# Feed-forward in 18 tiles of 256 tokens across batch borders, the first two interleaved, and one more head pair of batch 1 computed the early way

## The chip, the cores and the metric

The kernel runs on one NeuronCore of a Trainium2 chip. The core has five engines with queues of their own: TensorE (PE in the profile; its weight loads are shown apart as PEld), VectorE (DVE), ScalarE (ACT), GpSimd (POOL) and SyncE (SP), which here issues all DMA transfers. Each engine takes its instructions in the order in which they were put into its queue and waits for semaphores of the others. The metric is the device time of one execution in microseconds.

## The reference

There are three stages: attention of two kinds that are added, a low-rank mix along the sequence, and a feed-forward network. B = 8 batches, H = 8 heads, S = 576 positions, D = 64, so 512 channels.

```python
q_d, k_d, v_d = (t.reshape(B, H, S // 4, 4, D).mean(axis=3) for t in (q, k, v))
out_d = softmax(q_d @ k_d.T / sqrt(D)) @ v_d            # pooled by four
out_up = np.repeat(out_d, 4, axis=2)
out_local = softmax(where(|i - j| < 4, q @ k.T / sqrt(D), -1e9)) @ v   # window of 7
x = (out_up + out_local).transpose(0, 2, 1, 3).reshape(B, S, 512)
xt = x.transpose(0, 2, 1)
u = x + (xt @ U @ V).transpose(0, 2, 1)                 # U: 576x32, V: 32x576
out = u + relu(u @ w_ch1) @ w_ch2                       # 512 -> 2048 -> 512
```

(Shortened; the maximum is subtracted ahead of each exponential, and 1e-9 is added to each sum.) U, V and the two weight matrices come in as float64, which the kernel converts itself.

## The kernel before

**The plan.** The kernel doesn't issue instructions as it goes. It makes a list of operations (`op`, with an engine, an assumed duration, what is read and written, and a priority), and `Plan.run` plays the list through a small model of the engines, which then fixes the order in each queue. Lower priorities go first when an engine has a choice. A pair of heads `hp` of batch `b` has priority 10 (4b + hp) and up; feed-forward matmuls have FILL + step (1000 and up), so they fill TensorE where attention has nothing ready. PH and PF are the assumed durations of a feed-forward group of twelve and of three matmuls.

**Feed-forward.** Every number of the products is split in a high and a low part of type fp32r (uH, uL, hH, hL, W1H, W1L, W2H, W2L), and a product is three matmuls: high by high, low by high and high by low. The tokens of a batch are cut in two tiles of TN = 288. A *step* is one tile with one of the NFC = 16 chunks of 128 hidden channels. `ffn1` (L888) does 4 x 3 matmuls into `ps_h`; ScalarE makes hH = relu (L895), VectorE hL (L896). `ffn2` (L911), LAG = 3 steps later, does four groups of three matmuls into four accumulators, one PSUM bank for each quarter e of the 512 output channels. After the last chunk of a tile, POOL adds uH and uL (L921), VectorE adds the accumulator (L924), and four stores go out (L927). The steps run batch by batch, tile by tile, chunk by chunk.

**Weights.** `load_w1` and `load_w2` bring 16 raw chunks each; `convert` (L341 to L354) turns float64 bits to high and low float32 parts: two copies on ScalarE, four operations on VectorE (L342, L344, L347, L349), one on POOL. The raw chunks use the three buffers "Pt", which the late attention's products Pt (L799) use as well. W2 lives where the early attention had its buffers: the operation "late" releases them when all early operations are done, and the steps from the fourth on wait for it.

**Attention, two ways.** Pairs with b * HP + hp < NE = 5 (all four of batch 0, the first of batch 1) go *early*: scores, transposes and products with v all on TensorE (`early_global`, `local_blocks`), before W2 is there. Batch 0 then goes through `early_mix`; the pair of batch 1 stores its x to DRAM (x_s) and is mixed later. All other pairs go *late* (`late_global`, `local_attn`): the scores on TensorE are passed through DRAM to another layout, the product with v runs as POOL multiplications (L799) and VectorE sums (L804), and the result is stored as x_s (L806). `mix_part` reads x_s back twice (xL, Y), multiplies by U on TensorE (L848), then by V (L863, one matmul for each tile of tokens), adds x (L866) and writes uH (L869) and uL (L871) of that pair's 128 channels. A tile can start when all four pairs of its batch are mixed; uH and uL have two buffers each.

**Loops.** Early attention of batch 0 and the first pair of batch 1, then the weights, U, the mix of the held early pair, the rest of batch 1, then the steps. The attention of batch b + 1 is put into the list ahead of the first step of batch b; the order in the queues comes from the plan.

Of the kernel before, what the change touches and what calls it, by code (L numbers as in the profile page):

```python
# [201 lines left out]
def attn_mix_ffn_kernel(ctx: ExitStack, tc, q, kp, vp, qT, kT, v, U, Ub, V, w1, w2, mask, band, eye, pat, pool, vw, vn, ident, outT):  # L202
    nc = tc.nc
# [10 lines left out]
    TN = 288  # L214
    NT = S // TN
    R = V.shape[0] // 4
    MP, MJ = U.shape[0], U.shape[1] // R
    LAG = 3
# [3 lines left out]
    PH, PF = 1.587, 0.398  # L222
# [3 lines left out]
    NE = 5  # L226
# [48 lines left out]
    ident_sb = const.tile([128, 128], F32, name="ident_sb")  # L275
# [15 lines left out]

    band_sb = early_pool.tile([128, NS * KL], BF16, name="band_sb")
# [40 lines left out]
    dma(lambda: nc.sync.dma_start(out=mask_sb, in_=mask), [], ["mask"], 35, 32)  # L333

# [72 lines left out]

    heads = [slice(hh * D, (hh + 1) * D) for hh in range(2)]
# [86 lines left out]
    def late_global(b, hp, up_s, prio):  # L495
# [39 lines left out]
        def t_mm():  # L535
            for hh in range(2):
                for c in range(2):
                    for a in range(2):
                        nc.tensor.transpose(view(pt[hh])[:, c, a * QH:(a + 1) * QH],  # L539
                                            Es[hh]()[:, a, c * QH:(c + 1) * QH], ident_sb[:QH, :QH])  # L540
        op(PE, 0.52, t_mm, ek + ["ident"], pt, prio)
# [13 lines left out]
        od = g([QH, 4, D], "od")  # L555
# [114 lines left out]
    def early_mix(b, hp, x, prio):  # L670
# [14 lines left out]
        for t in range(NT):  # L685
            pu = psum(ps_m, "ps_u", "m:x", 2)
            cuts = [(r, max(t * TN, 128 * r), min((t + 1) * TN, 128 * (r + 1))) for r in range(NS)]
            cuts = [x for x in cuts if x[1] < x[2]]

            def um(t=t, pu=pu, cuts=cuts):  # L690
                tsl = slice(t * TN, (t + 1) * TN)
                nc.tensor.matmul(pu()[:, :TN], stk(), Vst[:, tsl], start=True, stop=False)
                for r, c0, c1 in cuts:
                    nc.tensor.matmul(pu()[:, c0 - t * TN:c1 - t * TN], flat(r), ident_sb[:, c0 - 128 * r:c1 - 128 * r],
                                     start=False, stop=(r == cuts[-1][0]))
            op(PE, pw(prio) * 1.05, um, rd + [(stk, 0), (stk, 1), (stk, 2), "ident", "V0H", "V1H", "V0L", "V1L"], [pu], prio)
            uH, uL = u_of(b, t)
            act(TN, lambda uH=uH, pu=pu: nc.scalar.activation(uH()[:, hp, :], pu()[:, :TN], AF.Copy),
                [pu], [(uH, hp)], prio, 0.05)
            dve(TN, lambda uH=uH, uL=uL, pu=pu: nc.vector.tensor_tensor(  # L700
                out=uL()[:, hp, :], in0=pu()[:, :TN], in1=uH()[:, hp, :].bitcast(F32), op=ALU.subtract),
                [pu, (uH, hp)], [(uL, hp)], prio)
# [106 lines left out]
    u_bufs = {}  # L809

    def u_of(b, t):
        if (b, t) not in u_bufs:
# [238 lines left out]
```

## Time and profile before

| | us |
|---|---|
| three runs, median (lowest to highest) | 1037.83 (1037.47 to 1038.42) |
| the profiled execution: span from first to last instruction | 1036.6 |
| TensorE busy | 996.9 |
| POOL busy | 557.2 |
| VectorE busy | 529.8 |
| ScalarE busy | 388.0 |

The profile is of one execution, with the span as its own time; the medians of the runs are a little above it. In the tables of groups, a row gives source line, engine, operation, the tile written and those read, the shapes, the count, the busy time in us and the mean of one in ns, and then the time for which the engine sat idle just before these instructions, with what ended it. In a timeline a row is start, duration (us), engine, line, operation, tiles, shapes, count. A row of a window gives from:to, length, then busy time and count of PE, PEld, DVE, ACT and POOL, then the granted TensorE clock (1.00 is full), the share of the DMA engines in use, and GB/s. The page's digits are tenths of 40 equal slices of the span. Matmuls are pipelined, so the duration of one is a latency: the distance from start to start tells what each costs.

### The profile page before, as it was taken

The numbers are of one execution on the slowest core, as the hardware profiler recorded it, in microseconds if no ns is written. First come the engines' busy times: TensorE is split into PE (matmuls) and PEld (weight loads), VectorE is DVE, ScalarE is ACT, GpSimd is POOL, SyncE is SP. The second block draws the span as 40 slices with busy tenths as digits, with TensorE's granted clock in tenths as the row PEclk, the third lists the DMA queues.
The fourth block names the chain that finished last, engine by engine and source line by source line (L and its number), as shares of the span: only waits on it lengthen the run. The fifth ranks groups of instructions, "written<-read, shape, count | busy, mean of one in ns | idle before, by whom it ended". The sixth has DMA issues, their size and how long they took to land.

```text
span 1036.6 us, 26946 instructions
## 1 busy us (share of the span) xinstructions
PE 996.9 (96%) x10831; PEld 975.3 (94%) x10831; DVE 529.8 (51%) x1054; ACT 388.0 (37%) x1234; POOL 557.2 (54%) x567
## 2 busy tenths in 40 slices
PE   6778898999999999999999999999999999999998
PEld 5667888999999999999999999999999999999998
DVE  5997898655554545444475344534652544211111
ACT  3676554442443434443344244423443232111110
POOL 4854568788575656565585638762765625211010
PEclk9896999999999999999999999999999999999999
DMA  8866764753555545545555355624644242000000
GB/s 279 226 172 179 199 186 116 149 138 104 135 137 115 141 113 132 128 86 146 120 137 125 87 132 133 143 75 101 151 116 117 64 113 50 24 1 24 1 24 23
DMA packets 222612, 120.30 MB, mean 116 GB/s; under 512 B 175492, under 2 KB 198456, under 8 KB 222488
## 3 DMA queue, kind: packets, MB, share of 16 engines
q1 hardware_dynamic: 222488, 118.58, 45.5%
q8 instruction: 85, 1.39, 0.6%
q14 instruction: 39, 0.32, 0.1%
HBM read 87.78 MB, written 30.75 MB: 114 GB/s over the span
## 4 chain that ended last, share of the span: by engine, by line
PE 84%; DVE 7%; POOL 3%; issue 2%; DMA 2%; ACT 2%; SPq 0%; DVEq 0%; POOLq 0%; ACTq 0%
PE acc L911 36%; PE ps_h L888 35%; PE ps_a L552 2%; PE ps_b L719 2%; DVE c L347 2%; PE ps_hu L848 1%; DVE c L349 1%; PE ps_t L539 1%; DMA w2r<-in_W 1%; PE ps_b L726 1%; POOL Pt L799 1%; DVE c L342 1%; DVE c L344 1%; PE ps_a L484 1%; PE ps_v L431 1%
## 5 line engine op out<-in xcount | busy, mean ns | idle before, releaser
L911 PE MATMUL acc<-hH,W2H 128*128 128x288 f32 x1024 | 310.5, 303 | 0.0
L896 DVE SCALAR_TENSOR_TENSOR hL<-ps_h,hH 128x288 fp32r<-128x288 f32 x256 | 116.6, 455 | 378.6 <-ACT hH L895 378.0
L888 PE MATMUL ps_h<-uH,W1H 128*128 128x288 f32 x1024 | 304.3, 297 | 4.1 <-DVE hL L896 3.1
L911 PE MATMUL acc<-hH,W2L 128*128 128x288 f32 x1024 | 303.1, 296 | 2.6 <-POOL W2L L354 2.6
L888 PE MATMUL ps_h<-uL,W1H 128*128 128x288 f32 x1024 | 303.4, 296 | 1.2 <-POOL uL L871 1.2
L911 PE MATMUL acc<-hL,W2H 128*128 128x288 f32 x1024 | 302.6, 296 | 0.0
L888 PE MATMUL ps_h<-uH,W1L 128*128 128x288 f32 x1024 | 302.0, 295 | 0.0
L799 POOL TENSOR_TENSOR Pt<-vl,at 128x896 f32<-128x896 f32 (+1 forms) x135 | 233.4, 1809 | 115.1 <-DVE acc L804 61.1
L895 ACT ACTIVATE hH<-ps_h 128x288 fp32r<-128x288 f32 x256 | 105.1, 410 | 433.6 <-PE ps_h L888 433.5
L888 PEld LDWEIGHTS ps_h<-uH,W1H 128*128 128x128 f32 x1024 | 193.5, 189 | 5.4 <-DVE hL L896 3.8
L911 PEld LDWEIGHTS acc<-hH,W2L 128*128 128x128 f32 x1024 | 193.2, 189 | 3.5 <-POOL W2L L354 3.5
L888 PEld LDWEIGHTS ps_h<-uL,W1H 128*128 128x128 f32 x1024 | 193.4, 189 | 1.5 <-POOL uL L871 1.5
L911 PEld LDWEIGHTS acc<-hH,W2H 128*128 128x128 f32 x1024 | 193.3, 189 | 1.1
L888 PEld LDWEIGHTS ps_h<-uH,W1L 128*128 128x128 f32 x1024 | 193.7, 189 | 0.0
L911 PEld LDWEIGHTS acc<-hL,W2H 128*128 128x128 f32 x1024 | 193.7, 189 | 0.0
L804 DVE TENSOR_REDUCE acc<-Pt 128x128 f32<-128x1024 f32 (+1 forms) x135 | 144.7, 1103 | 4.7 <-POOL Pt L799 2.3
L871 POOL TENSOR_TENSOR uL<-xT,uH 128x288 fp32r<-128x288 f32 x56 | 44.1, 811 | 71.3 <-ACT uH L869 71.2
L921 POOL TENSOR_TENSOR o<-uH,uL 128x288 f32<-128x288 f32 x64 | 49.8, 816 | 54.2 <-DMA out_t<-o 54.2
L840 POOL TENSOR_TENSOR xL<-xL,xH 116x640 fp32r<-116x640 f32 x28 | 44.0, 1572 | 64.2 <-ACT xH L839 49.3
L510 POOL TENSOR_TENSOR vr<-vr 72x256 f32<-72x256 f32 x54 | 42.4, 785 | 46.9 <-DMA vr<-in_v 46.8
L793 ACT ACTIVATE Pt<-ul 128x128 f32<-128x128 f32 (+1 forms) x135 | 48.4, 441 | 21.3 <-DVE acc L804 20.0
L744 ACT ACTIVATE se<-ps_b 96x114 f32<-96x114 f32 x108 | 38.5, 357 | 47.1 <-PE ps_b L719 34.1
(129 smaller groups left out, 1106.9 us busy)
## 6 DMA issues: line engine op xcount, KB each, us to landing
vl<-in_vp SPq DMA_DIRECT2D x54, 240.0 KB
out_t<-o SPq DMA_DIRECT2D x64, 144.0 KB
w1r<-in_W SPq DMA_DIRECT2D x16, 512.0 KB
w2r<-in_W SPq DMA_DIRECT2D x16, 512.0 KB
Y<-x_s SPq DMA_DIRECT2D x112, 72.0 KB
gT<-in_kT SPq DMA_DIRECT2D x27, 291.0 KB
xL<-x_s SPq DMA_DIRECT2D x28, 280.0 KB
gq<-in_qT SPq DMA_DIRECT2D x27, 288.0 KB
```

Of the source, the lines that this page charges most:

```text
L510: pool_tt(256, lambda x=x: nc.gpsimd.tensor_tensor(out=x()[:, :, 0:2, :], in0=x()[:, :, 0:2, :], in1=x()[:, :, 2:4, :], op=ALU.add), [x], ...
L744: act(n * KL, lambda p=ps[hh], se=se, n=n, rows=rows: nc.scalar.activation(se()[rows, 0:n].rearrange("p r k -> p (r k)"), p()[rows, 0:n * ...
L793: act(n * D, lambda n=n, ps=ps, Pt=Pt: nc.scalar.activation(Pt()[:, :n, :, 7], ul()[:, ps, :], AF.Copy), [ul], [(Pt, 1)], prio, 0.16)
L799: nc.gpsimd.tensor_tensor(out=Pt()[:, :n, :, 0:7].rearrange("p s d o -> p o s d"), in0=win, in1=at()[:, ps, :].rearrange("p s o -> p o s") ...
L804: dve(8.5 * n * D, lambda n=n, ps=ps, Pt=Pt: nc.vector.tensor_reduce(out=acc()[:, ps, :], in_=Pt()[:, :n], axis=AX.X, op=ALU.add), [(Pt, 0 ...
L840: pool_tt(640, lambda: nc.gpsimd.tensor_tensor(out=xL(), in0=xL().bitcast(F32), in1=xH().bitcast(F32), op=ALU.subtract), [xL, xH], [xL], prio)
L871: pool_tt(TN, lambda uH=uH, uL=uL, uf=uf: nc.gpsimd.tensor_tensor(out=uL()[:, hp, :], in0=uf(), in1=uH()[:, hp, :].bitcast(F32), op=ALU.su ...
L888: nc.tensor.matmul(ps()[:, :TN], w[:, dc, fs], u()[:, dc, :], start=(n == 0), stop=(n == 3 * NDC - 1))
L895: last_h[i] = act(TN, lambda: nc.scalar.activation(hH(), ps()[:, :TN], AF.Relu), [ps], [hH], FIRST, 0.05)
L896: dve(TN, lambda: nc.vector.scalar_tensor_tensor(hL(), ps()[:, :TN], 0.0, hH().bitcast(F32), op0=ALU.max, op1=ALU.subtract), [ps, hH], [hL ...
L911: nc.tensor.matmul(ac[e]()[:, :TN], W2[w][:, fc, es], hx(), start=(fc == 0 and n == 0), stop=(fc == NFC - 1 and n == 2))
L921: pool_tt(TN, lambda e=e, o1=o1: nc.gpsimd.tensor_tensor(out=o1()[:, :TN], in0=uH()[:, e, :].bitcast(F32), in1=uL()[:, e, :].bitcast(F32), ...
```

## The change

TN becomes 256 and tiles are numbered through all 8 x 576 tokens, so there are NG = 18 tiles of 256 and a tile may hold tokens of two batches. A batch's mix therefore writes its u in three pieces (`pieces`), and a tile waits for every pair of each batch that it touches (`parts`). Two quarters of an output tile share one PSUM bank; tiles take turns between two pairs of banks. The steps of the first two tiles alternate chunk by chunk. NE becomes 6, so the second pair of batch 1 goes the early way. uH and uL get three buffers. The final adds work on two quarters at once, with half as many stores (the last tile still by quarters). The identity used by the late transposes is a small tile of its own (`id_late`), the full one moves into the early memory. The assumed durations are set anew.

```diff
-    TN = 288
-    NT = S // TN
+    TN = 256
+    NG = B * S // TN
+    FIRST_TILES = 2
-    LAG = 3
+    LAG, HLB = 3, 3
-    PH, PF = 1.587, 0.398
+    PH, PF = 1.36, 0.34
-    NE = 5
+    NE = 6
-    ident_sb = const.tile([128, 128], F32, name="ident_sb")
+    id_late = const.tile([QH, QH], F32, name="id_late")
+    ident_sb = early_pool.tile([128, 128], F32, name="ident_sb")
+    dma(lambda: nc.sync.dma_start(out=id_late, in_=ident[0:QH, 0:QH]), [], ["id_late"], 35, 21)
+    def u_of(g):
+        if g not in u_bufs:
+            u_bufs[g] = (buf(ffn, [128, NDC, TN], F32R, "uH", bufs=3), buf(ffn, [128, NDC, TN], F32R, "uL", bufs=3))
+        return u_bufs[g]
+    def pieces(b):
+        cuts = [b * S] + [x for x in range(0, B * S, TN) if b * S < x < (b + 1) * S] + [(b + 1) * S]
+        return [(x // TN, x - b * S, y - x, x % TN) for x, y in zip(cuts, cuts[1:])]
+    parts = {}
+    for b in range(B):
+        for g, _, _, _ in pieces(b):
+            parts.setdefault(g, []).append(b)
...
-        for t in range(NT):
-            tsl = slice(t * TN, (t + 1) * TN)
+        for g, c, n, off in pieces(b):
             pu = psum(ps_m, "ps_u", "m:x", 2)
...
-            op(PE, 0.14, um, [(stk, 0), (stk, 1), (stk, 2), "V0H", "V1H", "V0L", "V1L"], [pu], prio)
+            op(PE, 0.13, um, [(stk, 0), (stk, 1), (stk, 2), "V0H", "V1H", "V0L", "V1L"], [pu], prio)
...
     def ffn1(s, i):
-        b, t, fc = s
-        uH, uL = u_of(b, t)
+        g, fc = s
+        uH, uL = u_of(g)
...
+        ur = [(u, c, b) for u in (uH, uL) for c in range(NDC) for b in parts[g]]
+        op(PE, PH, mm, ur + [f"W1_{fc}H", f"W1_{fc}L"] + ["late"] * (i >= HLB), [ps], FILL + i)
...
     def ffn2(s, i):
...
-            accs[(b, t)] = [psum(ps_acc, f"acc{e}", f"acc{e}", 1) for e in range(NDC)]
-        ac = accs[(b, t)]
+            accs[g] = [psum(ps_acc, f"acc{e}", f"acc{2 * (g % 2) + e}", 1) for e in range(NDC // 2)]
+        ac = accs[g]
+        half = lambda e: ac[e // 2]()[:, (e % 2) * TN:(e % 2 + 1) * TN]
...
-                    nc.tensor.matmul(ac[e]()[:, :TN], W2[w][:, fc, es], hx(),
-                                     start=(fc == 0 and n == 0), stop=(fc == NFC - 1 and n == 2))
+                    nc.tensor.matmul(half(e), W2[w][:, fc, es], hx(), start=(fc == 0 and n == 0 and e % 2 == 0),
+                                     stop=(fc == NFC - 1 and n == 2 and e % 2 == 1))
...
-    steps = [(b, t, fc) for b in range(B) for t in range(NT) for fc in range(NFC)]
+    first = [(g, fc) for fc in range(NFC) for g in range(FIRST_TILES)]
+    steps = first + [(g, fc) for g in range(FIRST_TILES, NG) for fc in range(NFC)]
...
+    for b in range(2, B):
+        attention(b)
     for i in range(len(steps) + LAG):
         if i < len(steps):
-            b, t, fc = steps[i]
-            if t == 0 and fc == 0 and b > 0 and b + 1 < B:
-                attention(b + 1)
             ffn1(steps[i], i)
```

105 lines of the change are left out of this document (51 added, 54 removed).

## The prediction

> **What bounds the kernel now.** I read the page first, for the engine that is busy and for the slices in which it isn't.
>
> ```profile
> PE 996.9 (96%) x10831; PEld 975.3 (94%) x10831; DVE 529.8 (51%) x1054; ACT 388.0 (37%) x1234; POOL 557.2 (54%) x567
> PE   6778898999999999999999999999999999999998
> DVE  5997898655554545444475344534652544211111
> PE acc L911 36%; PE ps_h L888 35%; PE ps_a L552 2%; PE ps_b L719 2%; DVE c L347 2%; PE ps_hu L848 1%; DVE c L349 1%; PE ps_t L539 1%; DMA w2r<-in_W 1%; PE ps_b L726 1%; POOL Pt L799 1%; DVE c L342 1%; DVE c L344 1%; PE ps_a L484 1%; PE ps_v L431 1%
> L911 PE MATMUL acc<-hH,W2H 128*128 128x288 f32 x1024 | 310.5, 303 | 0.0
> L888 PE MATMUL ps_h<-uH,W1H 128*128 128x288 f32 x1024 | 304.3, 297 | 4.1 <-DVE hL L896 3.1
> ```
>
> The chain that ended last is TensorE, 71% of it in the two feed-forward lines. Each line has three such groups of 1024, so the feed-forward is 6144 matmuls. The 303 and 297 ns are latencies of overlapped matmuls; what one costs is the distance between starts. For that I took the timeline in a stretch without attention, and a window that shows its clock:
>
> ```profile
> 959.81 0.29 PE L888 MATMUL ps_h<-uH,W1H 128*128 128x288 f32 x1
> ...
> 961.40 0.29 PE L911 MATMUL acc<-hH,W2H 128*128 128x288 f32 x1
> 950.00:1000.00 50.00, 50.00 (x380) 50.00 (x379) 8.32 (x19) 6.46 (x16) 3.14 (x4) 1.00 0.04 13
> ```
>
> Twelve matmuls lie between these starts: 1.59 us / 12 = 132.4 ns each, at a granted clock of 1.00 (in a window's row the third number from the right), while the other engines are nearly idle. So 6144 x 0.1324 = 813.5 us of the span of 1036.6 are feed-forward. The rest is the beginning and the attention's own matmuls.
>
> The second view is that beginning. Steps (a tile with one of the 16 weight chunks) 0 to 31 are the two tiles of batch 0; step 32 is the first that needs batch 1.
>
> ```profile
> L895 ACT ACTIVATE hH<-ps_h x32: 387/408/441, 85.0 to 223.7; 128x288 fp32r<-128x288 f32 x32
> L659 ACT ACTIVATE ob<-ps_ba x10: 418/431/438, 43.4 to 91.6; 128x320 f32<-128x320 f32 x10
> L351 ACTq EVENT_SEMAPHORE  x3: 17/38/38, 99.1 to 99.4; - x3
> L354 POOL TENSOR_TENSOR W2L<-c,W2H x16: 1263/1312/3420, 100.7 to 165.1; 128x512 fp32r<-128x512 f32 x16
> 105.00:165.00 60.00, 54.06 (x577) 51.43 (x576) 54.62 (x91) 31.55 (x87) 37.42 (x32) 0.97 0.65 182
> 195.06 0.52 SPq L806 DMA_DIRECT2D x_s<-acc  x1
> 209.72 0.34 SPq L806 DMA_DIRECT2D x_s<-acc  x1
> 229.35 0.29 PE L888 MATMUL ps_h<-uH,W1H 128*128 128x288 f32 x1
> 232.06 0.40 PE L888 MATMUL ps_h<-uL,W1H 128*128 128x288 f32 x1 [1.23 <-POOL uL L871]
> ```
>
> The early attention ends at 91.6; its memory is free for W2 at about 99. W2 is converted until 165.1, with VectorE busy 54.62 of 60 us. The raw weights and the attention's products Pt share three buffers, so the late pairs of batch 1 come through behind the weights: the second stores its x_s at 195.06, the third and last at 209.72. Step 32 starts at 229.35 (the 33rd hH follows the 32 above) and waits 1.23 us inside for uL. Up to here 32 steps of L888 and, with the lag of three, 29 of L911 are issued: 61 x 12 = 732 matmuls. The other 5412 x 0.1324 = 716.5 us; 1036.6 - 229.35 - 716.5 = 90.7 us are the late pairs from then on, their switches, and the end.
>
> So the sum for the new kernel has three terms: the start of step 32, the matmuls left (18 x 384 = 6912, less 732 = 6180) by their cadence, and some 91 us of others.
>
> **Term 1, the cadence at 256 columns.** The trace has no matmul of this shape. What stands near it:
>
> ```profile
> 92.43 0.44 PE L888 MATMUL ps_h<-uH,W1L 128*128 128x288 f32 x1
> 92.67 0.44 PE L888 MATMUL ps_h<-uH,W1H 128*128 128x288 f32 x1
> 92.19:94.59 2.40, 2.40 (x11) 2.40 (x11) 1.88 (x3) 0.98 (x4) 2.24 (x4) 0.50 0.55 149
> 891.76 0.46 PE L848 MATMUL ps_hu<-xH,Ust 116*64 116x128 f32 x5
> 892.06 0.46 PE L848 MATMUL ps_hu<-xL,Ust 116*64 116x128 f32 x5
> L888 PEld LDWEIGHTS ps_h<-uH,W1H 128*128 128x128 f32 x1024 | 193.5, 189 | 5.4 <-DVE hL L896 3.8 <-ACT ob L659 1.3
> L848 PEld LDWEIGHTS ps_hu<-xH,Ust 116*64 116x64 f32 x140 | 12.5, 135 | 2.7 <-POOL Ust L354 2.7
> ```
>
> At half the clock a matmul of 288 columns takes exactly 0.24 us, so 288 columns at full clock are 120 ns and 256 are 106.7; the measured 132.4 has a surplus of 12.4. A weight load of 128 columns takes 189 ns, of 64 columns 135: 54 ns per 64 columns, 108 per 128. L848 has 64 columns of weights and 128 of data and takes 0.30 us / 5 = 60 ns, 6 over its load of 54 and 7 over its columns (53.3). The new shape is L848 with both streams doubled: load 108, columns 106.7. From below 108 ns (a load per matmul), from above 106.7 + 12.4 = 119.1 (the surplus of 288 stays). Between them lies the line through 60 ns at 128 and 132.4 at 288: 0.4525 ns per column, 117.9 at 256. I take **114**: 108 + 6, as L848, the one row in which load and columns stand in the same proportion as in the new shape. 6180 x 0.114 = **704.5 us**.
>
> **Term 2, the start of step 32.** Three edits act here. *Two tiles together* gives TensorE two steps for every W2 chunk. *The second pair of batch 1 goes early*: one late pair less behind the weights. *Smaller tiles* shorten its 732 matmuls by 732 x 18 ns = 13 us.
>
> The extra early pair delays the release. Ten ob in five pairs from 43.4 to 91.6 is 12 us a pair at most (weight conversions ran between); I take 10, so W2 may be written from 109. Its VectorE work, from the groups of the first 210 us:
>
> ```profile
> L804 DVE TENSOR_REDUCE acc<-Pt 128x128 f32<-128x1024 f32 (+1 forms) x15 | 16.3, 1100 | 1.3 <-POOL Pt L799 1.1
> L451 DVE TENSOR_REDUCE mx<-ps_s 72x2 f32<-72x288 f32 x10 | 4.1, 446 | 2.3 <-PE ps_s L444 2.3
> L620 DVE TENSOR_REDUCE nm<-ps_b 128x5 f32<-128x190 f32 x10 | 3.2, 343 | 3.1 <-PE ps_b L600 3.1
> L622 DVE TENSOR_TENSOR ms_b<-ps_b,nm 128x190 f32<-128x190 f32 x10 | 3.2, 342 | 0.0
> L628 DVE TENSOR_REDUCE rs_b<-ms_b 128x10 f32<-128x380 f32 x5 | 2.7, 538 | 0.6 <-ACT ms_b L627 0.6
> L487 DVE TENSOR_TENSOR od<-ps_a,ri 72x128 f32<-72x128 f32 x10 | 2.8, 276 | 3.7 <-PE ps_a L484 3.6
> ```
>
> Two each of L451, L620, L622, L487 and one L628: 3.4 us, against 5 x 1.1 = 5.5 us of L804 alone for the late pair that goes. VectorE, the engine that limits the conversions, thus has no more to do; three chunks can be converted before the release, and only a little of the 10 us reaches the end of W2. Its loads and stores replace those of the late pair; the DMA engines' share was 0.65 in 105 to 165 (second number from the right in that window's row): hidden, and with that cover gone a few us of the same delay.
>
> Now batch 1's last pair is the second behind the weights: 195.06 + 1 for the later W2 + 21 from store to use (209.72 to 229.35, and the 1.23 waited) = **217**. TensorE alone would be there sooner: 109 + (732 - 36) x 0.114 = 188, plus three or four late pairs by the 90.7 us / 24 pairs = 3.8 us each, some 203. So what is late next is the attention, and TensorE waits up to 14 us, part of which other pairs' matmuls fill. Ends: 205 and 229 (nothing gained).
>
> **Term 3, the others.** 90.7 without the wait of 1.2; each of some 24 pairs gets three pieces of u instead of two (64, 128 and 192 columns among them): one more matmul, 108 to 132 ns by the rows above, 24 x 0.11 = 2.6: **92.1 us**. The third add, copy and subtract of each pair fall on engines at 51, 37 and 54%; the feed-forward covers them, and without that cover each pair would be under 2 us later. The accumulators of two tiles in turn remove a wait at the tile's border that the page shows as 0.0: nothing. The outputs (38 stores for 64, one wide add for two) and the smaller identity: nothing, TensorE goes on beside them. The last tile still stores by quarters: nothing.
>
> Two later places are tight. A tile then lasts 384 x 0.114 + 92.1 / 16 = 49.5 us. Tile 4 needs batch 2 at 217 + 99 = 316, tile 6 batch 3 at 415.
>
> ```profile
> L806 SPq DMA_DIRECT2D x_s<-acc x7: 337/344/530, 177.7 to 303.6; - x7
> L806 SPq DMA_DIRECT2D x_s<-acc x11: 332/344/530, 177.7 to 410.9; - x11
> ```
>
> Four pairs took 209.7 to 303.6, the next four to 410.9. From 196 on: batch 2 by 290 + 21 = 311, batch 3 by 397 + 21 = 418. That is cover of 5 us and a want of 3; a feed-forward step that waits there stands ahead of the attention's matmuls in TensorE's queue. From tile 9 on (564 against some 525) there is cover. I leave it at nothing and put it into the range.
>
> **Sum.** 217 + 704.5 + 92.1 = 1013.6 us of span. The median of the runs, 1037.83, is 1.2 over the profiled span: **1015 us**.
>
> **The rivals.**
>
> *A, the surplus stays (slower).* If the 12.4 ns belong to the matmul and not to its columns, 768 more matmuls pay them too: cadence 119.1, 6180 x 0.1191 = 736.0, span 1045.1, time **1046**. The place is every feed-forward matmul, and it decides from (1036.6 - 217 - 92.1) / 6180 = 117.7 ns on. For it: the cold row shows that columns alone cost 120. Against it: L848 has a surplus of 7. The Trainium skill, "TensorE: Matmul & The Clock Gate", section "Back-to-back issue gap", has this form, columns by the clock plus a constant 2.5 ns; the trace agrees with the columns at half clock and not with the constant (12.4), so its form speaks against the change and its size isn't this kernel's.
>
> *B, the line through the two rows.* 117.9 x 6180 = 728.6, span 1037.7, time **1039**. For it: two rows and no further assumption; against it: L848 may be paced by its load. This is the rival that I hold strongest, and it lies on the border of no change.
>
> *C, step 32 isn't earlier.* If the release and the weights slip as much as the pair saves, it stays at 229: 229 + 704.5 + 92.1, time **1027**. It is also what comes out when two tiles together do not fill TensorE. For it: VectorE has little room in 105 to 165.
>
> **Chances.** Forecast 0.56 (its own range 1002 to 1024, from step 32 at 205 to 225 and 112 to 115 ns), C 0.12, B 0.2, A 0.1, others 0.02. A measurement of this kernel can tell about 0.2%, 2 us, from none. Forecast and C are faster; B falls a quarter below 1035.8, a third within, the rest above; A is slower. Faster 0.74, same 0.07, slower 0.19. The range reaches from the forecast's lower end with a little more for the cadence's floor to B with some delay: 998 to 1043.
>
> **What would show it.** The distance of starts in L888 and L911 after attention has ended: 114 holds the forecast, 118 or more turns it. The first hH of tile 2 at about 217, with a wait on uL or uH before it and W2's last conversion at 165 to 170. Between 110 and 200 the steps of two tiles alternate and TensorE shows few gaps. Waits of L888 on the mix near 316 and 415, if the attention lags. I am wrong in size if the cadence is off by 1 ns (6.2 us), and in sign if it exceeds 117.7.

## The result and the profile after

The changed kernel takes **1066.23 us** in the median of four runs (1064.91 to 1070.98), the kernel before 1037.65 beside it: a ratio of **1.0277**, 95% interval 1.0247 to 1.0307. It is slower, and 51 us over the forecast. The profiled execution after has a span of 1062.7 us, so its median lies 3.5 us above it (1.2 before). One run of `plan_real_durations` (3340.61 us, its others 1069 to 1074) and one of the kernel before beside it (1899.37) stand far apart from the rest and are left out below.

The page of the kernel after: busy time, two rows of slices, and one group of each feed-forward line. ffn1 is now L899, ffn2 L923, hH L906, hL L907, ob L677.

```profile
PE 1004.9 (95%) x11706; PEld 984.8 (93%) x11706; DVE 532.2 (50%) x1088; ACT 398.5 (38%) x1294; POOL 539.8 (51%) x559
PE   5777498999999999999999999999999999999998
DVE  6887299665555544444445454645454443211111
L923 PE MATMUL acc<-hH,W2H 128*128 128x256 f32 x1152 | 332.9, 289 | 0.0
L899 PE MATMUL ps_h<-uH,W1H 128*128 128x256 f32 x1152 | 326.3, 283 | 2.2 <-DVE hL L907 2.2
```

TensorE is as full as before from the sixth slice on, and the feed-forward waits 2.2 us in all. The fifth slice shows a hole, a 4, with VectorE at 2. Both losses can be read from two further views. First the cadence, in the timeline of after where attention has ended:

```profile
954.35 0.28 PE L923 MATMUL acc<-hH,W2H 128*128 128x256 f32 x1
...
955.79 0.28 PE L899 MATMUL ps_h<-uH,W1H 128*128 128x256 f32 x1
...
957.20 0.28 PE L923 MATMUL acc<-hH,W2H 128*128 128x256 f32 x1
```

Twelve matmuls of L923 take 1.44 us, 120.0 ns each; twelve of L899 take 1.41, 117.5. Over all distances under 130 ns from step 32 on the means are 119.7 and 117.4, together 118.54, against 114 in the sum.

Second the beginning, by tiles of after (the third row answers for the first 245 us), with the start of step 32 from the timeline:

```profile
L677 ACT ACTIVATE ob<-ps_ba x12: 421/432/437, 41.4 to 117.7; 128x320 f32<-128x320 f32 x12
L354 ACT ACTIVATE W2H<-c x16: 612/632/637, 126.6 to 181.7; 128x512 fp32r<-128x512 f32 x16
L906 ACT ACTIVATE hH<-ps_h x35: 357/383/442, 86.6 to 241.3; 128x256 fp32r<-128x256 f32 x35
235.39 0.28 PE L899 MATMUL ps_h<-uH,W1H 128*128 128x256 f32 x1
```

The last early pair ends at 117.7 instead of 91.6, W2's first chunk is written at 126.6 instead of 100.0, and step 32 starts at 235.39, 6 us later than before and 18 later than forecast. The hole is the stretch from 105 to 128, in the windows of before and then of after:

```profile
105.00:128.00 23.00, 19.96 (x156) 19.11 (x155) 18.63 (x32) 11.79 (x33) 12.33 (x12) 0.99 0.76 213
```

```profile
105.00:128.00 23.00, 7.97 (x204) 6.84 (x205) 6.38 (x16) 7.45 (x25) 5.86 (x9) 0.50 0.68 166
127.00:235.00 108.00, 102.51 (x1154) 100.69 (x1147) 85.37 (x153) 57.00 (x171) 76.63 (x70) 0.99 0.59 149
```

TensorE and VectorE, at 20 and 18.6 us of these 23 before, now come to 8 and 6.4, and the granted clock stands at 0.50 (0.99 before). From 127 to 235 TensorE is nearly full again (102.5 of 108 us), so the delay stays. What the sixth pair waits for is in SyncE's part of the timeline of after, where a row's count is DMAs in a row and its length the time to issue them:

```profile
101.93 1.11 SPq L509 DMA_DIRECT2D up_e<-od  x2
...
106.06 3.22 SPq L845 DMA_DIRECT2D Y<-x_s  x4
109.40 2.23 SPq L400 DMA_DIRECT2D w2r<-in_W  x1
111.67 0.70 SPq L604 DMA_DIRECT2D vw<-up_e  x2
112.48 3.98 SPq L770 DMA_DIRECT2D s_s<-se  x8
...
121.75 1.36 SPq L683 DMA_DIRECT2D x_s<-ob  x1
```

and in TensorE's and ScalarE's (idle time before an instruction in brackets):

```profile
115.62 1.78 PE L673 MATMUL ps_ba<-vw,et 46*32 46x64 f32 x80 [4.31 <-DMA vw<-up_e]
125.69 0.26 ACT L794 ACTIVATE ms<-ms 128x63 f32<-128x63 f32 x1 [7.51 <-DVE ms L791]
126.55 1.67 ACT L354 ACTIVATE W2H<-c 128x512 fp32r<-128x512 f32 x3
```

The pair's intermediate goes out through DRAM (up_e, 101.93) and is read back at 111.67, behind other transfers in the one queue; ob follows at 117, its stores at 121.75 behind eight s_s and more. ScalarE meanwhile stands at ms of a late pair until 125.69, with W2H queued behind it.

At the other end of the delay stands batch 1's last late pair, the second behind the weights. Its store to x_s in SyncE's timeline, and in POOL's the last uL that step 32 needs (the first of the two in the row, 0.60 us long):

```profile
208.62 0.34 SPq L824 DMA_DIRECT2D x_s<-acc  x1
234.02 1.29 POOL L882 TENSOR_TENSOR uL<-xT,uH 128x192 fp32r<-128x192 f32 x2 [0.93 <-ACT uH L880]
```

So attention was ready at 234.6 and TensorE came to step 32 at 235.39: the two ended together.

By the terms of the forecast the span is now 235.4 + 6180 x 118.54 ns (732.6) + others 94.7 = 1062.7. Against the forecast that is **+18.4 for step 32, +28.1 for the cadence, +2.6 for the rest**; against before +6.0, +16.1 and +4.0.

### The profile page after: what moved, and what is told of

Same layout as the page of the kernel before. It is cut to its first block, busy times and chain, and to the rows that moved or that the text cites. A ratio compares the mean times of both kernels' runs of the same rounds, so it can differ in the third digit from the quotient of the medians.

```text
span 1062.7 us, 28743 instructions
## 1 busy us (share of the span) xinstructions
PE 1004.9 (95%) x11706; PEld 984.8 (93%) x11706; DVE 532.2 (50%) x1088; ACT 398.5 (38%) x1294; POOL 539.8 (51%) x559
## 4 chain that ended last, share of the span: by engine, by line
PE 86%; DVE 7%; DMA 4%; ACT 2%; issue 1%; SPq 1%; POOL 0%; DVEq 0%; ACTq 0%; POOLq 0%
PE acc L923 37%; PE ps_h L899 37%; PE ps_a L570 2%; PE ps_b L737 2%; PE ps_hu L860 2%; DVE c L350 2%; PE ps_t L557 1%; PE ps_b L744 1%; DVE c L352 1%; PE ps_u L874 1%; PE ps_v L449 1%; DMA vl<-in_vp 1%; DVE c L345 1%; DVE c L347 1%; DMA pool_sb<-in_pool 1%
## 5 line engine op out<-in xcount | busy, mean ns | idle before, releaser
L923 PE MATMUL acc<-hH,W2H 128*128 128x256 f32 x1152 | 332.9, 289 | 0.0
L899 PE MATMUL ps_h<-uH,W1H 128*128 128x256 f32 x1152 | 326.3, 283 | 2.2 <-DVE hL L907 2.2
L923 PE MATMUL acc<-hL,W2H 128*128 128x256 f32 x1152 | 325.5, 283 | 0.0
L923 PE MATMUL acc<-hH,W2L 128*128 128x256 f32 x1152 | 325.1, 282 | 0.0
L899 PE MATMUL ps_h<-uH,W1L 128*128 128x256 f32 x1152 | 324.3, 281 | 0.0
L899 PE MATMUL ps_h<-uL,W1H 128*128 128x256 f32 x1152 | 323.9, 281 | 0.0
L907 DVE SCALAR_TENSOR_TENSOR hL<-ps_h,hH 128x256 fp32r<-128x256 f32 x288 | 121.6, 422 | 398.0 <-ACT hH L906 395.9
L906 ACT ACTIVATE hH<-ps_h 128x256 fp32r<-128x256 f32 x288 | 110.1, 382 | 424.3 <-PE ps_h L899 412.2
L899 PEld LDWEIGHTS ps_h<-uH,W1H 128*128 128x128 f32 x1152 | 221.3, 192 | 3.1 <-DVE hL L907 2.6
L923 PEld LDWEIGHTS acc<-hH,W2H 128*128 128x128 f32 x1152 | 220.2, 191 | 0.8
L923 PEld LDWEIGHTS acc<-hL,W2H 128*128 128x128 f32 x1152 | 220.3, 191 | 0.0
L923 PEld LDWEIGHTS acc<-hH,W2L 128*128 128x128 f32 x1152 | 220.2, 191 | 0.0
L899 PEld LDWEIGHTS ps_h<-uL,W1H 128*128 128x128 f32 x1152 | 217.5, 189 | 0.0
L899 PEld LDWEIGHTS ps_h<-uH,W1L 128*128 128x128 f32 x1152 | 217.1, 188 | 0.0
L932 POOL TENSOR_TENSOR o<-uH,uL 128x512 f32<-128x512 f32 x36 | 45.8, 1293 | 90.9 <-DVE hL L907 90.9
L882 POOL TENSOR_TENSOR uL<-xT,uH 128x256 fp32r<-128x256 f32 (+3 forms) x84 | 48.9, 602 | 56.7 <-ACT uH L880 56.6
```

What stands on the lines that cost most here:

```text
L882: pool_tt(n, lambda uH=uH, uL=uL, uf=uf, n=n, off=off: nc.gpsimd.tensor_tensor(out=uL()[:, hp, off:off + n], in0=uf(), in1=uH()[:, hp, off ...
L899: nc.tensor.matmul(ps()[:, :TN], w[:, dc, fs], u()[:, dc, :], start=(n == 0), stop=(n == 3 * NDC - 1))
L906: last_h[i] = act(TN, lambda: nc.scalar.activation(hH(), ps()[:, :TN], AF.Relu), [ps], [hH], FIRST, 0.05)
L907: dve(TN, lambda: nc.vector.scalar_tensor_tensor(hL(), ps()[:, :TN], 0.0, hH().bitcast(F32), op0=ALU.max, op1=ALU.subtract), [ps, hH], [hL ...
L923: nc.tensor.matmul(half(e), W2[w][:, fc, es], hx(), start=(fc == 0 and n == 0 and e % 2 == 0), stop=(fc == NFC - 1 and n == 2 and e % 2 == 1))
L932: pool_tt(2 * TN, lambda e0=e0, v2=v2: nc.gpsimd.tensor_tensor(out=v2(), in0=uH()[:, e0:e0 + 2, :].bitcast(F32), in1=uL()[:, e0:e0 + 2, :] ...
```

## The experiments

The theory after the result had two halves: the extra early pair delays the release by its trips through SyncE's queue, and a matmul of 256 columns costs 118 to 120 ns whatever is done. The rivals were the interleaving of two tiles, the plan's priorities and assumed durations, and something particular to this kernel that slows a matmul which could run at 113.

**The parts of the change, one at a time.** `one_early_pair` takes the sixth pair back, `one_first_tile` the interleaving, `tiles_only` both; `before_six_early` puts the sixth pair alone into the kernel before.

```diff
-    NE = 6            # one_early_pair, tiles_only; the reverse, 5 to 6, in before_six_early
+    NE = 5
-    FIRST_TILES = 2   # one_first_tile, tiles_only
+    FIRST_TILES = 1
```

> The changed kernel with NE = 5, so the second pair of batch 1 is late again. Theory (the sixth early pair holds back the release of the memory for W2 by some 27 us): first write of W2H back at about 100 instead of 126.6, step 32 at 215 to 229 instead of 235.4, time 1046 to 1060. Rival (the pair is neutral, since the third late pair behind the weights takes what the release gives): step 32 at 235 or later, time 1064 to 1070.

> The changed kernel with FIRST_TILES = 1, so the first two tiles follow one another. Theory (two steps for each W2 chunk keep TensorE busy while W2 is converted): first write of W2H stays at about 126, step 32 moves from 235 to about 250, time about 1080. Rival (TensorE is not short of work there, alternation is worth nothing): 1064 to 1070.

> The kernel before with NE = 6 alone, tiles of 288. Theory (the sixth early pair holds back W2, and TensorE, over 90% busy from there to step 32, has no room to make it up): first write of W2H at 110 to 126 instead of 100, time 1042 to 1060. Rival (the late pair that is saved pays for it): 1030 to 1039.

> The changed kernel with FIRST_TILES = 1 and NE = 5: tiles of 256 across the borders, alternating accumulators and the rest, but neither of the two early edits. If the two edits add up (one_early_pair +10.5, one_first_tile -3.8): 1073. Theory (with five early pairs batch 1 comes too late for step 32 whatever the order of the first tiles): 1070 to 1077. Rival (the two edits were the harm, tiles are neutral): 1035 to 1045.

| | us | ratio to before, 95% |
|---|---|---|
| one_early_pair | 1076.73 | 1.0373 (1.0350 to 1.0396) |
| one_first_tile | 1062.40 | 1.0238 (1.0213 to 1.0263) |
| before_six_early | 1054.17 | 1.0151 (1.0119 to 1.0182) |
| tiles_only | 1078.65 | 1.0387 (1.0360 to 1.0415) |

The sixth pair costs 16 us in the kernel before, where neither tile size nor order changed. Its tiles there:

```profile
L659 ACT ACTIVATE ob<-ps_ba x12: 415/430/437, 41.6 to 114.9; 128x320 f32<-128x320 f32 x12
L351 ACT ACTIVATE W2H<-c x16: 613/632/637, 124.4 to 180.9; 128x512 fp32r<-128x512 f32 x16
```

W2 is written from 124.4, nearly as late as in the changed kernel, and step 32 starts at 247.6 instead of 229.35: in the kernel before, the delay belongs to the pair, as that run's expectation had it. But with the new tiles, taking it back is 10 us slower still. W2 then starts at 111.1, so the pair is 15 of the changed kernel's 27 us there, and the other 11 came with other parts of the change. TensorE now waits elsewhere, for the late pairs of batches 1 to 3. The waits of TensorE in 205 to 460 of `one_early_pair`, with total, times and longest:

```profile
PE ps_u L874 <- DVE stk L865: 7.3, 3, 3.9
PE ps_hu L860 <- POOL xL L852: 3.6, 1, 3.6
PE ps_u L874 <- DVE xT L877: 3.0, 3, 1.6
```

13.9 us, where the changed kernel has 2.3 in the two L874 rows of this view. In the trace they lie just ahead of step 32 (6.1 us), of tile 4 (3.3) and of tile 6 (4.4), and they cost more than their length: in 218 to 233 the granted clock averages 0.80. So the sixth pair exchanges a wait at the release for waits at step 32 and at tiles 4 and 6, the two places that the forecast called tight. The first expectation (release is all) fell for that reason; `tiles_only` came within 2 us of its own. The interleaving was expected to be worth time. Without it the kernel is not slower (4 us faster here, with intervals that overlap, and 0.3 slower in the pair of runs with pads below), with W2H from 125.9 for 126.6: it gives nothing.

**The plan.** `pair_sooner` gives the early pairs of batch 1 a better priority; `plan_real_durations` gives the plan's assumed step durations by what was measured.

```diff
-            p = 10.0 * (b * HP + hp)
+            p = 10.0 * (b * HP + hp) - 12.0 * (b == 1 and hp < NE - HP)   # pair_sooner
-    PH, PF = 1.36, 0.34
+    PH, PF = 1.41, 0.36                                                   # plan_real_durations
```

> The changed kernel with both early pairs of batch 1 12 priority points ahead, so before the last W1 conversions and under the limit from which waits are planned longer. Theory (the release is late because the sixth pair's chain runs alone at the end, with its transfers queued on SP behind others): first write of W2H at 105 to 112, step 32 at 215 to 220, time 1044 to 1052. Rival (the early stage as a whole is short of VectorE or DMA, order doesn't matter): first write stays beyond 120, time 1062 to 1070.

> The changed kernel with PH, PF = 1.41, 0.36, about what the profile shows for its twelve and three matmuls (12 x 117.2 and 3 x 119.9 ns), instead of 1.36, 0.34. Theory (the order was planned for matmuls 4% too fast, so work of the attention stands at the wrong places): time 1050 to 1060. Rival (the cadence itself is the cost, the order fits as well as before): 1063 to 1069.

1065.48 us (1.0266, 1.0237 to 1.0296) and 1071.44 (1.0331, 1.0285 to 1.0377). The first moved W2H from 126.6 to 124.9 and step 32 from 235.4 to 233.6, and the time not; the second made it worse. Both theories fell (the first run's rival came true, the second run lies above its rival as well): neither of these two settings is the cause.

**The release.** `held_pair_on_act_queue` issues the sixth pair's read of vw and its stores from ScalarE instead of SyncE; `before_release_sooner` frees the early memory of the kernel before without waiting for its last pair's x_s stores.

```diff
+        eng = nc.scalar if prio == 50.0 else nc.sync                     # held_pair_on_act_queue
-            dma(lambda hh=hh: nc.sync.dma_start(
+            dma(lambda hh=hh: eng.dma_start(
...
-        ob = buf(early_pool, [128, NS, 2, D], F32, "ob", None, 2)        # before_release_sooner
+        ob = buf(early_pool if x_s is None else loc, [128, NS, 2, D], F32, "ob", "ob" if x_s is None else "obl", 2 if x_s is None else 1)
...
-    early_ops = list(plan.ops)
+    early_ops = [o for o in plan.ops if o not in puts]
```

> The changed kernel, where the sixth pair's read of up_e and its stores to x_s are issued by ScalarE and not by SyncE. Theory (the sixth pair's chain is held by SyncE's queue, 8 us ahead of the read and 4 ahead of the stores): first write of W2H at 112 to 117 instead of 126.6, step 32 at 222 to 228 instead of 235.4, time 1053 to 1060. Rival (the chain is as long without it, by its landings and engines): 122 to 127, time 1063 to 1068.

> The kernel before, where the held pair's ob lies in another pool and the release of the early memory doesn't wait for its stores to x_s. Theory (the release sets when W2 and with it step 32 come): first write of W2H at 92 to 95 instead of 100, step 32 some 3 to 6 us sooner, time 1032 to 1035. Rival (step 32 is set by batch 1's late pairs, through VectorE and POOL): step 32 stays near 229, time 1036 to 1039.

1071.39 us (1.0321, 1.0293 to 1.0350) and 1038.88 (1.0008, 0.9990 to 1.0027). In the first the stores did come sooner, but W2 didn't, as its ScalarE timeline shows:

```profile
119.33 0.54 ACTq L687 DMA_DIRECT2D x_s<-ob  x1
129.62 0.26 ACT L797 ACTIVATE ms<-ms 128x63 f32<-128x63 f32 x1 [11.64 <-DVE ms L794]
130.40 1.68 ACT L354 ACTIVATE W2H<-c 128x512 fp32r<-128x512 f32 x3
```

The last store is issued at 119.33 (124.35 in the changed kernel), and ScalarE then stands 11.64 us at ms of a late pair, which is ahead of W2H in its queue and whose data still come through SyncE. In the second W2H starts at 99.7, as without the edit. The store is one of several things that end together there; removing one of them buys nothing. So the traces show where the pair waits, but no run here made the release earlier with six early pairs, and that SyncE's queue is the whole of the delay is not shown.

**The matmul by itself.** Rows of 48 matmuls appended to the kernel before, after its last tile (their time comes on top and isn't compared); shortened:

```diff
+            for i in range(48):
+                w = (W1H, W1H, W1L)[i % 3][:, i % NDC, (i % NFC) * 128:(i % NFC) * 128 + cols]
+                x = W2[("H", "L", "H")[i % 3]][:, i % NFC, shift:shift + n]
+                nc.tensor.matmul(ps()[:cols, off:off + n], w, x, start=(i == 0), stop=(i == 47))
```

> The kernel before with rows of 48 matmuls of one shape each appended behind its work (their results are not used), so its own time is longer by them. Measured is the distance of starts. Theory (line): the cost follows the columns, 0.4525 ns each plus 2.5, whatever the weights: 128 columns 60, 256 columns 118, 288 132, 512 234 ns, and 256 columns with 64 columns of weights also 118. Rival (load): the weight load of 108 ns sets a floor and adds some 6: 256 columns 114 to 118 with 128 weights but about 109 with 64 weights, and 64 to 192 columns all about 110 with 128 weights. Rival (fixed surplus of 12): 256 columns 119, 512 columns 226, 128 columns 66 to 110. A difference between the two halves of a PSUM bank (rows pn and phalf at 256 columns) of some 2.5 ns would explain why L923 takes 119.9 and L899 117.2.

First and last matmul of the rows of 224, 256 and 288 columns, in its timeline:

```profile
1058.55 0.28 PE L994 MATMUL pn<-W2H,W1H 128*128 128x224 f32 x1
...
1063.82 0.27 PE L994 MATMUL pn<-W2H,W1L 128*128 128x224 f32 x1
1063.92 0.29 PE L994 MATMUL pn<-W2H,W1H 128*128 128x256 f32 x1
...
1069.46 0.28 PE L994 MATMUL pn<-W2H,W1L 128*128 128x256 f32 x1
1069.58 0.29 PE L994 MATMUL pn<-W2H,W1H 128*128 128x288 f32 x1
...
1075.84 0.30 PE L994 MATMUL pn<-W2H,W1L 128*128 128x288 f32 x1
```

Over 47 distances: 112.1, 117.9 and 133.2 ns. From the starts of the other rows in the trace: 146.6 at 320, 176.7 at 384, 202.2 at 448, 233.4 at 512, and 109.9 at 64; the rows of 128 and 192 fell into a stretch of half the granted clock and are left out. Rival B's line through 60 and 132.4 (0.4525 ns a column) holds from 288 up: 233.4 - 133.2 over 224 columns is 0.447. Below it there is a floor of about 112 with 128 columns of weights. That the floor goes with the load is shown by rows with 64 columns of weights: 60.1 ns at 128 columns, 131.6 at 288, and at 256 (first and last of 48)

```profile
1135.26 0.28 PE L994 MATMUL pc<-W2H,W1H 128*64 128x256 f32 x1
...
1140.85 0.28 PE L994 MATMUL pc<-W2H,W1L 128*64 128x256 f32 x1
```

118.9 ns. With half the load, 256 columns are no cheaper: the load rival, which gave about 109 here, fell at this point, and the line held. So the load alone doesn't set the pace at 256 columns. With the full load the rows there didn't agree: one in the second half of a bank ran at 113.4, one with shifted data at 117.8, with the same instructions. Two further sets of rows asked what decides.

> The kernel before with rows of 48 matmuls of 256 columns appended behind its work (results not used). In the first probe such rows took 113.4 ns (second half of a bank; the same weights each time) or 117.9 (others), each locked to a short pattern, and the changed kernel's tail 117.2 (L899) and 119.9 (L923). Theory (phase: loads of 107 ns and columns of 107 ns run beside one another and lock in one of several patterns; which one depends on how the row is entered): rows with a lead matmul of 32 to 192 columns ahead (ph to pm) differ in their pattern, equal rows (pb and pc) may differ too. Rival (addresses: the half of the bank or the operands decide): pb and pc both 113.4, pa, pd and all rows with a lead the same as each other, pe 113.4, pg a mixture.

> The kernel before with rows of matmuls of 256 and 288 columns appended (results not used). pa, pe: 48 in a row, W1 as weights and W2 as data; pb: W2 as weights, W1 as data; pc, pd: V as data; pf, pg: eight groups of 12 into alternating banks, each read by ScalarE as in L899, so with a wait between groups; ph to pj the same at 288. Theory (the pattern is lost at each wait and found anew by chance): pa to pe 113.4 or 117.8 throughout, pf and pg 117 to 120. Rival (the operands decide, since L923, whose weights are W2, takes 120 and L899 117): pb and pc 120, pa and pd 113.4, pf as pa and pg as pb. At 288 all rows 132 to 133.

The first varied the bank's half, the weights and a single matmul put ahead of the row; the second the operands, and groups of 12 that ScalarE reads. One tile row each, with first and last start of 16: from `probe_modes` behind a lead of 96 columns (pj) and of 128 (pk),

```profile
L993 PE MATMUL pj<-W2H,W1L x16: 276/276/281, 1089.6 to 1094.7; 128*128 128x256 f32 x16
L993 PE MATMUL pk<-W2H,W1L x16: 281/281/281, 1095.2 to 1100.5; 128*128 128x256 f32 x16
```

and from `probe_waits` Vst as data, with W2 (pc) and with W1 (pd) as weights:

```profile
L993 PE MATMUL pc<-Vst,W2L x16: 276/276/278, 1055.6 to 1060.7; 128*128 128x256 f32 x16
L993 PE MATMUL pd<-Vst,W1L x16: 283/283/283, 1061.0 to 1066.4; 128*128 128x256 f32 x16
```

Over 45 distances these are 113.3 and 117.8, 113.3 and 120.0. All rows without a lead in these two sets ran at 113.3, except pd. So did the groups of 12, but TensorE never stood between them (no distance over 115 ns), so what a wait does is not shown. The way a row is entered chooses between 113.3 and 117.8 (two rows of `probe_columns` had 117.8 to 117.9 without a lead, so a lead is not the only such way), and something in pd gives 120, the number of L923. What pd has in common with L923 is the place. First byte of the tiles in a partition, modulo 128, from the kernels' own allocation:

```
                       W1   Vst    u   hidden   W2
before and the probes  32    32   96     96     96     pd: W1 with Vst, 0 apart; pc: W2 with Vst, 64 apart
after                  64    64    0      0      0     L899: W1 with u, 64 apart; L923: W2 with hidden, 0 apart
pad_before_w2          64    64    0      0     64     both 64 apart
pad_before_u           64    64   64     64     64     both 0 apart
pads_of_32             64    64   32     32     64     both 32 apart
```

**The place.** Padding only; what lies behind a pad moves by it:

```diff
+            w2p.tile([128, 16], F32, name="pad")     # pad_before_w2; 8 wide in pads_of_32
             W2["H"] = w2p.tile([128, NFC, DM], F32R, name="W2H")
...
     ffn = ctx.enter_context(tc.tile_pool(name="ffn", bufs=1))
+    ffn.tile([128, 16], F32, name="pad")             # pad_before_u; 8 wide in pads_of_32
```

> The changed kernel with a pad of 64 bytes per partition ahead of the resident W2, so that W2's columns and the hidden tiles that are multiplied with them no longer begin at the same place modulo 128 bytes (they do in the changed kernel; the up-projection's weights and data are 64 bytes apart already). Nothing else differs. Theory of places (a load that begins at the same place modulo 128 bytes as the data costs the 120 ns pattern, as the one probe row that had it did): the down-projection's matmuls go from 119.9 ns to 113 to 117.8, the up-projection's stay at 117.2; 3456 matmuls in the tail at 2 to 6.6 ns less give 1043 to 1059 us. Rival (the pattern is set by how each row of matmuls is entered, not by places): both cadences stay, 1063 to 1069 us.

> The opposite edit: the same pad ahead of the feed-forward's tiles, so that u, the hidden tiles and W2 all move by 64 bytes. Now u begins at the same place modulo 128 bytes as W1, and the hidden tiles still do as W2. Theory of places: the up-projection goes from 117.2 to 120 ns, the down-projection stays at 119.9; about 2700 matmuls at 2.8 ns more are 7.6 us, 1071 to 1076 us. Rival (places don't matter): 1063 to 1069 us.

> The changed kernel with 32 bytes per partition of padding ahead of the feed-forward's tiles and 32 more ahead of W2, so that W1 and u, and W2 and the hidden tiles, differ by 32 bytes modulo 128 (by 64 in pad_before_w2, whose tail ran at 117.6 and 117.7 ns and whose earlier part for the most part at 113). If a difference of 64 is still half a common place, the tail comes to 113.3 ns: 6180 matmuls at 4 to 5 ns less than 118.5 are 25 to 32 us, 1032 to 1042 us. Rival (64 is as good as 32, and the 117.7 ns of the tail come from the way a row is entered): 1043 to 1049 us, as pad_before_w2 did.

> The same pads, and one tile first in place of two together (one_first_tile was 4 us below the changed kernel). First theory: 1028 to 1038 us. Rival: 1039 to 1045 us.

> The kernel before with the same two pads. Its 288 columns take longer than a weight load (132.3 and 132.5 ns in its tail), so if only the load depends on the place, nothing changes: 1036 to 1039 us. If the data's reading suffers from the common place too, its matmuls lose up to 1 ns: 1030 to 1035 us.

Mean distances of starts in ns, worked out from the traces (250 to 850 us, with attention; from 850 on, mostly without), distances of 150 and over left out:

| | us | ratio to before, 95% | L899, L923 to 850 | from 850 |
|---|---|---|---|---|
| after | 1066.23 | 1.0277 (1.0247 to 1.0307) | 117.4, 119.6 | 117.7, 119.9 |
| pad_before_w2 | 1045.87 | 1.0072 (1.0040 to 1.0103) | 114.2, 114.8 | 117.6, 117.7 |
| pad_before_u | 1078.04 | 1.0366 (1.0326 to 1.0406) | 119.9, 119.7 | 120.0, 120.0 |
| pads_of_32 | 1064.46 | 1.0251 (1.0231 to 1.0272) | 118.3, 118.4 | 118.3, 118.7 |
| pads_of_32_one_first | 1064.78 | 1.0258 (1.0220 to 1.0296) | 118.3, 118.4 | 118.3, 118.7 |
| before_pads_of_32 | 1038.04 | 1.0005 (0.9988 to 1.0023) | 132.3, 132.8 | 132.3, 132.8 |

(The means of `pad_before_w2` are of the fastest of its five runs, 1040.86 us; the slowest took 1050.28.) 64 bytes of padding are worth 20 us, and the same bytes in the other place cost 12 (some 8 in the cadence, the rest in a later step 32). This is the theory of places, in both directions: at a common place the distance is 120 ns. Whether the load or the data is slowed by it is not shown. One part of the expectation missed: the up-projection, whose place was not touched, was to stay at 117.2, and up to 850 it fell to 114.2, which is a good third of the gain. The two stretches in the timeline of `pad_before_w2` (its lines are one higher), twelve matmuls each:

```profile
600.47 0.28 PE L924 MATMUL acc<-hH,W2H 128*128 128x256 f32 x1
...
601.83 0.28 PE L900 MATMUL ps_h<-uH,W1H 128*128 128x256 f32 x1
...
955.30 0.28 PE L900 MATMUL ps_h<-uH,W1H 128*128 128x256 f32 x1
...
956.72 0.28 PE L924 MATMUL acc<-hH,W2H 128*128 128x256 f32 x1
```

113.3 at 600 and 118.3 at 955, the pattern of probe rows entered well and badly. The whole trace says the same: from step 32 on, `pad_before_w2` has 52 stretches of at least 24 feed-forward distances with no other matmul and none of 130 ns or more between. 42 of them run at 113.3 and 10 at 117.8, and none changes its pattern inside. Attention's matmuls come between the stretches; they end at 881, and all that is left is one stretch that was entered at 117.8. The expectation that 32 bytes would do better than 64 fell: a fifth of the distances then lie at 122 to 150 ns. And the kernel before doesn't care: with the pads its distances stay at 132.3 and 132.8.

**The entry.** `pad_and_lead_in` adds to `pad_before_w2` a matmul of 96 columns ahead of the up-projection in 2 of 16 chunks; `pad_lead_in_one_first` has one tile first besides.

```diff
+            if fc % 8 == 1:
+                nc.tensor.matmul(ps()[:, :96], W1H[:, 0, fs], uH()[:, 0, :96], start=True, stop=True)
```

> pad_before_w2 with one added matmul of 96 columns ahead of the first matmul of the up-projection in 2 of a tile's 16 chunks (36 in all; what it writes is overwritten by the next one). In the probe, rows entered behind 96 or 192 columns ran at 113.3 ns and rows entered behind 32, 64, 128 or 160 at 117.8. The tail of pad_before_w2 stays at 117.8 from about 850 us on, without leaving it. If the entry sets the pattern and it holds until something breaks it: the tail runs at 113.3 to 115 ns, and the whole feed-forward nearer to 113.3: 1031 to 1042 us, the added matmuls (36 times 0.11 = 4 us) included. Rival (the tail's pattern has another cause, and the entry does nothing): 1047 to 1053 us.

> The same with one tile first in place of two together, which by itself was 4 us below the changed kernel. If both act: 1027 to 1039 us, faster than the kernel before at the lower end; if the entry does nothing: 1042 to 1050 us.

1051.88 us (1.0134, 1.0085 to 1.0183) and 1050.01 (1.0090, 1.0062 to 1.0118), where the rivals had them, the second at the edge. In the first, the tail's means go from 117.6 and 117.7 to 116.0 and 116.0 ns, and before 850 us they rise from 114.2 and 114.8 to 115.1 and 115.4. One lead (the matmul of 96 columns) in its timeline:

```profile
956.47 0.21 PE L899 MATMUL ps_h<-uH,W1H 128*128 128x96 f32 x1
956.51 0.35 PE L902 MATMUL ps_h<-uH,W1H 128*128 128x256 f32 x1
956.70 0.28 PE L902 MATMUL ps_h<-uL,W1H 128*128 128x256 f32 x1
```

The lead and the matmul behind it take 0.23 us together, 0.115 more than one matmul: the price is what was allowed. What failed is the choice. Of the 12 stretches (counted as above) that begin behind a lead, 10 run at 117.8 and 2 at 113.3; of the other 46, 37 run at 113.3. So an entry does set the pattern and it does hold until the next interruption, but a lead of 96 columns that chose the faster one in the probe mostly chose the slower one here. Which entry gives which is open. No version run here beats the kernel before.

## Why the prediction was wrong

**Term 1, the cadence at 256 columns: the step that failed first, +28.1 us.** The forecast took 114 ns, "108 + 6, as L848"; the kernel's mean is 118.54. As a number 114 is near the fastest of three patterns, 113.3, which most undisturbed rows ran at. Its reason isn't borne out: with half the load the shape costs 118.9, so load plus 6 does not explain the cost, and the nearness is in part luck. The step's hidden assumption was that a shape has one cadence. In this kernel W2 and the hidden tiles begin at the same place modulo 128 bytes, and L923 pays 119.7; L899, 64 bytes apart, pays 117.4. `pad_before_w2` gives back 20 of the 28 us, which shows that the place and not the shape makes these; the other 8 are left in its mean of 115.3, mostly as stretches at 117.8. The trace of before couldn't show this, since at 288 columns the place makes no difference. The bound of 119.1 at the top was exceeded by L923. The forecast's own range, 1002 to 1024, is also narrower than its ends add up to: 205 with 112 ns gives 990, 225 with 115 ns 1029.

**The rivals on the cadence.** A (119.1) and B (117.9) both lie 0.6 ns from the measured mean, and A named the right point: 118.54 is beyond its 117.7 from which the change is slower. A's mechanism fell, since the surplus isn't constant: 224 columns take 112.1 and 512 take 233.4, where 12.4 over the columns gives 105.7 and 225.7. B's line is real from 288 up and, with half the load, at 256 (118.9) as well; with the full load 256 columns can also take 113.3, which the line doesn't allow. The Trainium skill, "TensorE: Matmul & The Clock Gate", section "Back-to-back issue gap", gives columns by the clock plus 2.5 ns as the gap of an isolated matmul; the probe's rows from 288 up give 0.447 ns per column where the 0.24 us of 288 columns at half the clock give 0.417, so neither its slope nor its constant is this kernel's.

**Term 2, the start of step 32: +18.4 us, and the second step that failed.** The forecast added 195.06 for the store of batch 1's last pair, 1 for the later W2, and 21 from store to use. The store came at 208.62, so the 1 was 13.6, and from store to step 32 it took 26.8. Three of its points:
- *10 us for the extra early pair.* W2 was written 27 us later than before (126.6 against about 99). The pair alone made 24 in the kernel before (124.4 against 100.0) and 15 in the changed one (126.6 against 111.1). The 12 us a pair came from the ten ob, eight of them of batch 0. The sixth pair goes out to DRAM and back through SyncE's queue, among the late pairs' transfers. The prediction counted its loads as hidden, by bandwidth, and not by their turn in the queue; the traces show the turns, though no run that moved them made W2 sooner.
- *Two tiles together give TensorE work.* Without it (`one_first_tile`) the kernel isn't slower, and step 32 starts at 235.9 all the same.
- *Attention is late next, TensorE would be there at 203.* TensorE was there at 235.39 and attention at 234.6. The hole of 105 to 128 lies in its 32 us of delay. In `before_six_early` the last uL for step 32 ends at 236.6 and step 32 starts only at 247.6: there it was TensorE alone that came late.

C (step 32 not earlier) had this right in direction: 235 is even 6 us beyond its 229.

**Term 3, the others:** 94.7 for 92.1; right to 3 us. With six early pairs tile 4 didn't stall and tile 6 by 2.3 us; with five they did, by 3.3 and 4.4, so the tight places were real and the sixth pair is their cover.

The sum's form held: with two terms measured, what is left for the third is near its forecast. With the cadence alone off, it would have been 1043, at the range's upper end; the release took it beyond.

## What to carry to other kernels

Columns saved are not time saved in proportion: from 288 to 224 columns the distance fell by 16%, where the columns fell by 22, and below that hardly at all. Before shrinking a tile, run a row of the new shape with the kernel's own tiles, and look where weights and data begin modulo 128 bytes. An operation that gates a release should be priced with its turn in every queue that it passes, and not by its work or by bandwidth alone. And a change of several parts is best run part by part: here one part cost 16 us by itself and covered a wait that another had made.

## What the runs showed of the hardware that wasn't expected

At 256 columns with loads of 128, the distance of matmuls locks at 113.3, 117.8 or 120.0 ns. 120.0 appears where weights and data begin at the same place modulo 128 bytes (pd, L923, both lines of `pad_before_u`). 64 bytes apart gives one of the other two, chosen when a stretch is entered and kept until it is interrupted (52 of 52 stretches in `pad_before_w2`). In the probe a lead of 96 or 192 columns entered the faster one, 32, 64, 128 or 160 the slower; in the kernel 96 entered the slower in 10 of 12 stretches. 32 bytes apart gives 118.3 with scattered longer distances. With loads of 64 columns, 256 columns take 118.9. Why the place counts, and what in an entry makes the choice, stays open. SyncE needed some 0.35 to 0.85 us to issue a DMA in a full queue (eight s_s in 3.98 us, four Y in 3.22, four up_s in 3.40), and in 105 to 125 us the sixth pair's read and stores stood behind such rows.
